# Issuing W1's first half ahead of the mirror matrices, and batch 1's row sums ahead of batch 2's loads, on GpSimd

## The chip, the cores and the metric

The kernel runs on one core of one Trainium2 chip. The metric is the device time of one execution in microseconds (us). The engines are named as in the profile: PE (TensorE matmuls), PEld (its weight loads), DVE (VectorE), ACT (ScalarE), POOL (GpSimd) and SP (SyncE, which here only issues DMAs).

## The reference, cut to what matters

```python
scores = (1 / sqrt(64)) * q @ k.T                # 8 batches, 12 heads, 448 rows, 64 columns
attn   = maximum(scores, 0) ** 2 / 448
x      = (attn @ v) laid out as (8, 448, 768)    # heads side by side
mixed  = real(fft(fft(x, axis=1), axis=2))       # Fourier mixing over rows and columns
u      = x + mixed
un     = (u - mean(u)) / sqrt(var(u) + 1e-6)     # per row, over 768 columns
out    = u + maximum(un @ w_ch1, 0) @ w_ch2      # w_ch1: 768 x 3072, w_ch2: 3072 x 768
```

All inputs and the output are float32; the kernel works in bfloat16 for the products.

## The kernel before, in words

**Stages.** For each batch the kernel forms scores and values in pairs of heads (lines 961, 829, 834), brings the result `x` into `xT`, folds it for the Fourier transform (lines 734 to 787), multiplies by cosine and sine tables along the columns (`mix`, line 1439) and along the rows (`mix_rows`, line 1251). `mix_rows` then adds `x` to the mixed rows: its inner generator `rows(i)` makes `u`, the mean and variance, and the normalised `un`. A half of 128 or 112 rows has two mirrored parts: `i = 0` is summed on DVE and `i = 1` on POOL (lines 1282 and 1284, two instructions each). For batch 1 `un` is made on ACT (line 1310), and then turned on PE against a unit or a mirror matrix (line 1212, `turn_rows`) into `unT`, the input of the feed-forward product. Batch 0 has a path of its own, `first_tail`, in which POOL makes `un` at line 1109 for three of the four parts; it needs the mirror matrix `rev` on PE.

**Feed-forward.** The rows of all batches are cut into groups. `ffn` multiplies a group by W1 (line 1937), applies the maximum (line 1924 on ACT, line 1922 on DVE) and multiplies by W2 (line 1965 for the first group, 1992 and 2078 later), with line 1630 adding the result into the output rows. The later groups reuse sums of weight blocks to save products (lines 1533, 1769, 2078). The first group's second product walks W2 in four quarters and needs each quarter's load.

**The order of the work.** All instructions of an engine run in the order in which a planner, `Streams.run`, lists them when the program is built. Each part of the work is a generator ("stream") that says with `need(engine, time, due times, buffers)` when its next step could start. The planner takes the stream with the least key:

```python
t = [self.engine[eng]] + [d.t if isinstance(d, Cell) else d for d in deps]
...
key = (ok is not None and not ok(), max(t) + HEAD.get((s[3], eng, phase), 0.0), s[1][eng != "PE"])
```

`s[3]` is the name of the generator, `phase` counts which of the planner times 48, 140, 290 and 440 us have passed on PE, and the last entry is a rank that settles equal keys. `HEAD` thus makes one kind of step look earlier than it is, in one phase, on one engine.

**POOL's list.** POOL issues all loads of q, k, v, W1 and W2 through the software DMA queue (q0 in the profile), in the order that `loading` spells out; the stores and reloads of `u`, the transposes and the output go through SP (q1). Before each load the planner waits for the landing of the load eight places back (`ring`), and so does the program itself, which has eight loads in flight at most:

```python
def ring():
    return [landed[-8] + 1.2] if len(landed) > 7 else []
```

A load of a group of four heads is one instruction at line 483 for each of q, k, v (the k and v tiles are called `kn` and `vn`), and two small ones at line 458 for the last quarter of the rows (`load_halves`). `load_w1(0)` and `load_w1(1)` issue six loads each at line 522, `load_w2` two at a time at line 533. Between the loads POOL also makes small constants: `mirrors` (lines 283 to 303) makes `rev`, the index vectors `back` for the mirrored stores of line 1348, and the matrix `order` that `halve` uses at line 415; `seq_table` (lines 365 to 373) makes the angles from which DVE and ACT make the row tables (lines 380 to 390).

Of the kernel before, what the change touches and what calls it, by code (L numbers as in the profile page):

```python
# [61 lines left out]

HEAD = {('attentions', 'PE', 2): -0.6, ('attentions', 'PE', 3): -0.6, ('attentions', 'PE', 4): 0.07, ('mix_rows', 'PE', 2): -0.05}
OVERLAP = {"ACT": 0.12, "DVE": 0.07}
STAGE = [1]
LATENCY = {"PE": 0.28, "ACT": 0.18, "DVE": 0.16, "POOL": 0.2, "SP": 0.1}
# [3 lines left out]
class Streams:  # L72
# [29 lines left out]
    def run(self):  # L102
        end = {}
        while self.streams:
# [10 lines left out]
            for s in self.streams:  # L115
# [6 lines left out]
                for p in set(bufs):  # L122
                    t.append(sorted(p.free)[bufs.count(p) - 1])
                key = (ok is not None and not ok(), max(t) + HEAD.get((s[3], eng, phase), 0.0), s[1][eng != "PE"])
                if best is None or key < best[0]:
# [24 lines left out]
def need(eng, dur, deps=(), bufs=(), ok=None):  # L150
    return eng, dur, list(deps), list(bufs), ok
# [26 lines left out]
def kernel(  # L178
# [21 lines left out]
    NG = H // HG  # L200
# [81 lines left out]
    def mirrors():  # L282
        order[0] = work.tile([128, 128], BF16, name="order", tag="qkr0", bufs=1)
        nc.gpsimd.memset(rev, 0.0)
        nc.gpsimd.affine_select(out=rev, in_=rev, compare_op=ALU.not_equal, fill=1.0,
                                base=-127, pattern=[[1, 128]], channel_multiplier=1)
        nc.gpsimd.iota(back[0], pattern=[[0, 1]], base=HS, channel_multiplier=-1)

        v = const.tile([128, 2], FP32, name="backv")
        nc.gpsimd.iota(v[:, 0:1], pattern=[[0, 1]], base=HS - 128, channel_multiplier=-1,  # L290
                       allow_small_or_imprecise_dtypes=True)
        nc.gpsimd.tensor_scalar(v[:, 1:2], v[:, 0:1], 0.0, float(UB), op0=ALU.is_lt, op1=ALU.mult)
        nc.gpsimd.tensor_tensor(v[:, 0:1], v[:, 0:1], v[:, 1:2], op=ALU.add)
        nc.gpsimd.tensor_copy(back[1], v[:, 0:1])
        for i in range(2):
            nc.gpsimd.iota(back2[i], pattern=[[0, 1]], base=HS - 2 + i, channel_multiplier=-2)
        nc.gpsimd.memset(order[0], 0.0)
        for i in range(2):
            n = EH - i
            nc.gpsimd.affine_select(out=order[0][:, i * EH:i * EH + n], in_=order[0][:, i * EH:i * EH + n],  # L300
                                    compare_op=ALU.not_equal, fill=1.0, base=-i, pattern=[[-2, n]],
                                    channel_multiplier=1)
        nc.gpsimd.tensor_scalar(order[0][:, EH - 1:EH], order[0][:, EH - 1:EH], 0.5, None, op0=ALU.mult)
# [56 lines left out]
    def seq_table():  # L360

        f = work.tile([128, 4 * KH], FP32, name="dfty", tag="uA", bufs=1)
        g = work.tile([128, 4 * KH], FP32, name="dfty", tag="uB", bufs=1)
        yield need("POOL", 0.55)
        nc.gpsimd.iota(drow[:, 0:2], pattern=[[128, 2]], base=0, channel_multiplier=1,
                       allow_small_or_imprecise_dtypes=True)
        nc.gpsimd.iota(dcol[:, 0:SX], pattern=[[1, SX]], base=0, channel_multiplier=0,
                       allow_small_or_imprecise_dtypes=True)
        yield need("POOL", 0.3)
        nc.gpsimd.tensor_scalar(drow[:, 0:2], drow[:, 0:2], 1.0 / S, None, op0=ALU.mult)  # L370
        for i in range(2):
            e = yield need("POOL", 0.45)
            nc.gpsimd.tensor_scalar(f[:, i * SX:(i + 1) * SX], dcol[:, 0:SX], drow[:, i:i + 1], None, op0=ALU.mult)
        f, g = f[:, 0:2 * SX], g[:, 0:2 * SX]
        sch.add(seq_sines(f, g, e + LATENCY["POOL"]), (0, 0.3))

    def seq_sines(f, g, e):

        e = yield need("DVE", 0.4, [e])
        nc.vector.tensor_scalar(g.bitcast(mybir.dt.int32), f, 1.0, None, op0=ALU.mult)  # L380
        yield need("DVE", 0.55)
        nc.vector.tensor_tensor(f, f, g.bitcast(mybir.dt.int32), op=ALU.subtract)
        e = yield need("DVE", 0.4)
        nc.vector.tensor_scalar(g.bitcast(mybir.dt.int32), f.bitcast(mybir.dt.int32), 0x7FFFFFFF, None,
                                op0=ALU.bitwise_and)
        flat = seq.rearrange("p t a s -> p t (a s)")
        for dst, y, sign, bias in ((flat[:, 0], g, -1, halfpi), (flat[:, 1], f, 1, zero_t),
                                   (nseq.rearrange("p a s -> p (a s)"), f, -1, zero_t)):
            e = yield need("ACT", act(2 * SX), [e + LATENCY["DVE"], last_relu])
            nc.scalar.activation(dst, y, AF.Sin, bias=bias, scale=sign * 2.0 * math.pi)  # L390
        seq_ready.t = nseq_ready.t = dft_ready.t = e + LATENCY["ACT"]
# [44 lines left out]
    def ring():  # L436
        return [landed[-8] + 1.2] if len(landed) > 7 else []
# [25 lines left out]
    def load_group(i, which=(0, 1, 2), parts=(0, 1)):  # L463

        b, g = divmod(i, NG)
        hs = slice(g * HG, (g + 1) * HG)
        for x, src in enumerate((q, k, v)):
            if x not in which:
                continue
            if 0 in parts:  # L470
                if b == 0 and x < 2:
                    e = yield need("POOL", 0.75, ring())
                    t = first_qk[x][:R, g] if x == 0 else first_qk[x][:, g]
                else:
                    e = yield need("POOL", 0.75, ring() if b < 3 else [], [BQ[x] if x == 2 else BQ[x][home(i)]])
                    t = (work.tile([R, HG, 4 * Dh], BF16, name="qn", tag=f"qn{home(i)}", bufs=1) if x == 0 else
                         kn_homes[home(i)] if x == 1 else vn_home[:, 3 * g * HG * Dh:3 * (g + 1) * HG * Dh])
                if x == 0:
                    to, j, rows = t, 4, S
                else:  # L480
                    to, j, rows = (t[:, :, 0:3 * Dh] if x == 1 else
                                   t.rearrange("p (h x) -> p h x", h=HG)), 3, KT
                nc.gpsimd.dma_start(out=to, in_=src[b, hs, 0:rows].rearrange("h (p j) d -> p h (j d)", j=j))  # L483
                loads[i][x] = None if x == 2 else t.rearrange("p h (j d) -> p j h d", j=4)
                landed.append(sch.dma(e, GRP * rows / S, 390e3, "sw"))
                arrive(i, x)
            if i == 0 and x == 1:
                e = yield need("POOL", 0.55)
                dft_indices()
                indices_ready.t = e + LATENCY["POOL"]  # L490
                yield need("POOL", 0.6)
                make_identity(nc, ident)
            if x and 1 in parts and (b > 0 or g == x - 1):
                yield from load_halves(b, g if b else 0, 1 if b else NG, x)
            if i == 2 and x == 2:
                yield need("POOL", 0.75)
                pads()
            if i == NG + 1 and x == 1 and 0 in parts:
                yield need("POOL", 3.6)
                mirrors()  # L500


    qk_left = Cell()
    kn_homes = [work.tile([128, HG, 4 * Dh], BF16, name="kn", tag=f"kn{i}", bufs=1) for i in range(QN)]
# [13 lines left out]
    def load_w1(hf):  # L518
        for m in range(MC):
            e = yield need("POOL", 0.6, ring())  # L520
            t = wpool.tile([128, FF // 2], BF16, name=f"w1_{m}_{hf}")
            nc.gpsimd.dma_start(
                out=t, in_=moe_w_ch1[m * 128:(m + 1) * 128, hf * (FF // 2):(hf + 1) * (FF // 2)])
            w1_sb[m][hf] = t
            done = sch.dma(e, 128 * FF * 2, 430e3, "sw")
            landed.append(done)
        w1_ready[hf].t = done
# [11 lines left out]
    def loading():  # L539
        for i in range(NG):  # L540
            yield from load_group(i)

        yield from load_group(NG, (0, 1))
        yield from load_group(NG + 1, (0, 1), (0,))
        yield from load_w1(0)
        yield from seq_table()
        yield from load_group(NG + 1, (1,), (1,))
        yield from load_w1(1)
        for i in (NG, NG + 1):
            yield from load_group(i, (2,), (0,))  # L550
        yield from load_halves(1, 0, 2, 2)
        yield from load_group(NG + 2, (0, 1))
        yield from load_w2(range(2))
        yield from load_group(NG + 2, (2,))
        yield from load_w2(range(2, 4))
        for i in range(2 * NG, B * NG):
            yield from load_group(i)
# [931 lines left out]
    rows = out.rearrange("b s d -> (b s) d")  # L1489
# [732 lines left out]
```

## Time and profile before

| | us |
|---|---|
| three runs | 570.31, 567.71, 572.16; median 570.31 |
| the profiled execution's own time | 570.35 |
| its span, first to last instruction | 568.4 |
| PE busy | 557.1 (98% of the span), granted clock 0.999 |
| DVE, ACT, POOL busy | 436.4, 318.4, 194.4 |
| software queue q0 | 33.63 MB, 44.1% of 16 engines' span |
| hardware queue q1 | 48.09 MB, 38.7% |

The span runs from the first to the last instruction of the program; 1.95 us of the execution's time lie outside it. PE is the engine that carries the span, and the columns of the views that matter below are: a start time in us from the span's start, a duration, the engine, the line and its tiles, and in brackets the engine's idle time before the instruction and what ended it.

### The profile page before, as it was taken

What the parts mean: (1) busy time and instruction counts of PE and PEld (TensorE: products, weight loads), DVE (VectorE), ACT (ScalarE), POOL (GpSimd) and SP (SyncE); (2) the same over time, 40 slices, a digit from 0 to 9 for tenths busy, and PEclk for the clock granted to TensorE, in tenths of its full rate; (3) what the DMA queues carried; (4) which work ended last, traced back from release to release, by engine and by line L of the source; (5) the groups of instructions that cost most, each with busy time, mean ns of one, the idle gap of its engine ahead of it and who ended that gap; (6) DMA issues with size and microseconds to landing.
All of it is one profiled execution on the core that took longest, in us unless ns stands there. A gap on an engine that the chain in (4) does not pass through costs nothing.

```text
span 568.4 us, 11147 instructions
## 1 busy us (share of the span) xinstructions
PE 557.1 (98%) x4171; PEld 350.0 (62%) x4171; DVE 436.4 (77%) x1015; ACT 318.4 (56%) x537; POOL 194.4 (34%) x281
## 2 busy tenths in 40 slices
PE   8999998899999999999999999999999999999997
PEld 4475555544455555546756756767678688668864
DVE  7977563887789977887998897878899957644762
ACT  6978762677745676676786647638615164015400
POOL 8965223524336234462445545322005000000000
PEclk9999999999999999999999999999999999999999
DMA  9999999999968987899799989957425421231012
GB/s 113 175 210 233 201 219 150 220 152 119 176 94 219 210 137 157 163 184 211 163 160 206 191 126 160 194 128 154 115 65 167 117 87 29 71 124 57 1 57 83
DMA packets 152688, 82.41 MB, mean 145 GB/s; under 512 B 118076, under 2 KB 147900, under 8 KB 152636
## 3 DMA queue, kind: packets, MB, share of 16 engines
q0 software_dynamic: 57056, 33.63, 44.1%
q1 hardware_dynamic: 95580, 48.09, 38.7%
q8 instruction: 32, 0.52, 0.4%
q14 instruction: 20, 0.16, 0.1%
HBM read 62.91 MB, written 26.25 MB: 157 GB/s over the span
## 4 chain that ended last, share of the span: by engine, by line
PE 87%; DMA 6%; DVE 2%; ACT 2%; POOL 1%; issue 1%; DVEq 0%; POOLq 0%; ACTq 0%
PE psF L1937 25%; PE psF L2078 21%; PE psS L1769 8%; PE psS L961 8%; DMA kn<-in_k_dram 6%; PE psS L2078 5%; PE psF L834 5%; PE psF L1992 4%; PE psS L1439 2%; PE psF L1769 2%; PE psF L1965 2%; PE psF L829 1%; PE psF L630 1%; PE psS L834 1%; PE psS L1247 1%
## 5 line engine op out<-in xcount | busy, mean ns | idle before, releaser
L1937 PE MATMUL psF<-unT,w 128*128 128x256 bf16 (+2 forms) x1152 | 165.3, 299 | 0.0
L974 ACT ACTIVATE sq<-psS 128x896 bf16<-128x896 f32 x168 | 144.1, 920 | 31.7 <-PE psS L961 31.4
L1937 PEld LDWEIGHTS <-w 128*128 128x128 bf16 x1152 | 110.9, 98 | 49.6 <-issue 5.2
L991 DVE TENSOR_TENSOR sq<-sq 128x896 bf16<-128x896 bf16 x144 | 89.4, 638 | 13.8 <-ACT sq L974 13.2
L2078 PEld LDWEIGHTS <-hT 128*128 128x128 bf16 x648 | 62.4, 98 | 44.2 <-issue 4.6
L1924 ACT ACTIVATE hT<-psF 128x512 bf16<-128x512 f32 (+2 forms) x121 | 59.6, 508 | 41.4 <-PE psF L1937 39.3
L1630 DVE TENSOR_TENSOR o<-psF,o 128x384 f32<-128x384 f32 (+1 forms) x78 | 42.6, 547 | 23.5 <-PE psF L2078 19.8
L2078 PE MATMUL psF<-w,hT 128*128 128x384 bf16 x336 | 59.9, 326 | 0.7 <-DVE o L1630 0.6
L961 PE MATMUL psS<-qkT 64*128 64x448 bf16 (+1 forms) x336 | 51.5, 355 | 0.4 <-DVE qkT L637 0.3
L1784 ACT COPY copies<-psS 128x256 f32<-128x256 f32 x57 | 19.9, 374 | 53.1 <-PE psS L1769 48.0
L696 DVE TENSOR_SCALAR xT<-psF 128x224 bf16<-128x224 f32 x60 | 20.6, 384 | 26.8 <-PE psF L834 26.8
L1282 POOL TENSOR_TENSOR u<-tp,xn 112x385 f32<-112x385 f32 (+2 forms) x14 | 14.3, 1019 | 72.9 <-DVE tp L1262 49.3
L483 POOL DMA_DIRECT2D qn<-in_q_dram x21 | 15.7, 747 | 58.9 <-DVE qkr L590 51.4
L834 PE MATMUL psF<-sq,vn 128*64 128x448 bf16 x246 | 33.0, 362 | 0.0
L961 PEld LDWEIGHTS <-qkT 64*128 64x128 bf16 (+1 forms) x336 | 12.9, 94 | 31.7 <-issue 26.4
L1769 PEld LDWEIGHTS <-w 128*128 128x128 bf16 x288 | 28.2, 98 | 4.7 <-issue 1.1
L458 POOL DMA_DIRECT2D kn<-in_k_dram x42 | 25.7, 621 | 12.1 <-DMA w<-in_moe_w_ch_dram 8.0
L1291 DVE BATCH_NORM_STATS2 stats<-u 112x6 f32<-112x384 f32 (+2 forms) x56 | 28.7, 543 | 0.9 <-POOL u L1282 0.7
L458 POOL DMA_DIRECT2D vn<-in_v_dram x42 | 26.1, 637 | 5.9 <-DMA w<-in_moe_w_ch_dram 5.1
L483 POOL DMA_DIRECT2D vn<-in_v_dram x24 | 18.9, 787 | 25.5 <-PE psS L961 25.4
L1310 ACT ACTIVATE un<-u,small 112x768 bf16<-112x768 f32 (+2 forms) x22 | 22.0, 1023 | 10.0 <-DVE small L1297 8.6
L1965 PE MATMUL psF<-w,hT 128*128 128x384 bf16 x144 | 24.9, 326 | 1.5 <-DMA w<-in_moe_w_ch_dram 1.5
(239 smaller groups left out, 936.6 us busy)
## 6 DMA issues: line engine op xcount, KB each, us to landing
out_dram<-o SPq DMA_DIRECT2D x55, 192.0 KB, 2.1
qn<-in_q_dram POOLq DMA_DIRECT2D x21, 224.0 KB, 5.1
vn<-in_v_dram POOLq DMA_DIRECT2D x24, 192.0 KB, 5.6
w<-in_moe_w_ch_dram POOLq DMA_DIRECT2D x12, 384.0 KB, 10.6
w<-in_moe_w_ch_dram POOLq DMA_DIRECT2D x4, 1152.0 KB, 22.6
kn<-in_k_dram POOLq DMA_DIRECT2D x21, 192.0 KB, 5.6
utop<-u SPq DMA_DIRECT2D x12, 336.0 KB, 3.1
o<-utop SPq DMA_DIRECT2D x16, 192.0 KB, 3.7
```

The costliest lines, as they stand in the source:

```text
L458: nc.gpsimd.dma_start(out=t[par * Dh:(par + 1) * Dh, par::2], in_=at)
L483: nc.gpsimd.dma_start(out=to, in_=src[b, hs, 0:rows].rearrange("h (p j) d -> p h (j d)", j=j))
L834: nc.tensor.matmul(av[h * Dh:(h + 1) * Dh, 0:S], lhsT=vn_home[:, at:at + Dh], rhs=sq[:, h, :], start=start, stop=stop, skip_group_check=True)
L961: nc.tensor.matmul(sc[:, h, 0:S].rearrange("k (c q) -> k c q", c=4), lhsT=flat[ps, k0:k0 + KB], rhs=qT[ps, pair], start=True, stop=True)
L974: nc.scalar.activation(r, sc[:, :, 0:S], AF.Relu)
L991: nc.vector.tensor_tensor(r, r, r, op=ALU.mult)
L1630: nc.vector.tensor_tensor(o[:, cols], pc[:, cols], o[:, cols], op=ALU.add)
L1769: nc.tensor.matmul(ps[:, 0:N], lhsT=lhs, rhs=rhs[:, m], start=(start and m == 0), stop=(stop and m == 2), skip_group_check=True)
L1924: nc.scalar.activation(hs, ps, AF.Relu)
L1937: nc.tensor.matmul(ph[:, i * N:(i + 1) * N], lhsT=w1_sb[m][hf][:, (jj + i) * 128:(jj + i + 1) * 128], rhs=unT[:, m, 0:N], start=(m == 0), ...
L1965: nc.tensor.matmul(pc[:, 0:DH], lhsT=block(j, c), rhs=w2(j, hf), start=(j == 0), stop=(j == JC - 1))
L2078: nc.tensor.matmul(pc[:, cols], lhsT=lhs[i], rhs=rhs[i][:, cols], start=(start and i == 0), stop=(i == KP - 1), skip_group_check=True)
```

## The change

It has two parts. `mirrors` is called from `loading` directly behind `load_w1(0)`, where before it was called from `load_group` ahead of it, behind the k load of batch 1's second group: POOL's thirteen instructions for the mirror matrices come behind W1's first six loads. And the steps named `rows` get a head of 1.5 us on POOL in phase 1, which covers the row sums of batch 1.

```diff
-HEAD = {..., ('mix_rows', 'PE', 2): -0.05}
+HEAD = {..., ('mix_rows', 'PE', 2): -0.05, ('rows', 'POOL', 1): -1.5}
@@ load_group
-            if i == NG + 1 and x == 1 and 0 in parts:
-                yield need("POOL", 3.6)
-                mirrors()
@@ loading
         yield from load_group(NG + 1, (0, 1), (0,))
         yield from load_w1(0)
+        yield need("POOL", 3.6)
+        mirrors()
         yield from seq_table()
         yield from load_group(NG + 1, (1,), (1,))
         yield from load_w1(1)
```

More of the change, by code (lines that the diff above doesn't have):

```diff
@@ L61, in give @@
         self.ids.append((when, self.tiles.pop(id(t))[1]))
[L65 removed]
+HEAD = {('attentions', 'PE', 2): -0.6, ('attentions', 'PE', 3): -0.6, ('attentions', 'PE', 4): 0.07, ('mix_rows', 'PE', 2): -0.05, ('rows', 'POOL', 1): -1.5}
 OVERLAP = {"ACT": 0.12, "DVE": 0.07}
```

## The prediction

> **What bounds the kernel now.** I read the page first (PE busy 557.1 of 568.4 us), then the windows view, cut where PE stands idle, then the timelines of PE, DVE, ACT and POOL in those stretches. In the windows the first number is the stretch, the second PE's busy time.
>
> ```profile
> 20.00:88.00 68.00, 67.32 (x575) 38.24 (x572) 47.44 (x117) 50.25 (x83) 32.59 (x51) 1.00 1.17 208
> 88.00:106.00 18.00, 14.92 (x100) 9.24 (x99) 10.03 (x25) 5.41 (x8) 11.93 (x17) 1.00 1.60 147
> 106.00:545.00 439.00, 437.59 (x3203) 280.73 (x3202) 353.87 (x817) 247.67 (x428) 131.67 (x163) 1.00 0.76 139
> ```
>
> PE is the bound at full granted clock, and the change takes no product away. Only PE's idle time can move: 0.68 us from 20 to 88, 3.08 from 88 to 106, 1.41 from 106 to 545. The 3.08 are two waits, in PE's timeline:
>
> ```profile
> 90.34 2.11 PE L1965 MATMUL psF<-w,hT 128*128 128x384 bf16 x12 [1.51 <-DMA w<-in_moe_w_ch_dram]
> 93.62 9.91 PE L1965 MATMUL psF<-w,hT 128*128 128x384 bf16 x60
> 105.10 0.51 PE L1212 MATMUL psS<-ident,un 128*128 128x128 bf16 x6 [1.57 <-ACT un L1310]
> ```
>
> The first group's second product waits 1.51 us for the last quarter of W2. Then `turn_rows` waits 1.57 us for batch 1's first `un`, with a product behind it that needs nothing from it. Each part of the change lies upstream of one of these waits.
>
> **First part: W1 ahead of the mirrors.** POOL's timeline, and the DMA issues that start in stretches around single loads (last number: us from issue to landing):
>
> ```profile
> 17.43 0.82 POOL L483 DMA_DIRECT2D kn<-in_k_dram  x1
> 18.17 0.29 POOL L284 MEMSET rev<- 128x128 bf16 x1
> 21.01 3.33 POOL L522 DMA_DIRECT2D w<-in_moe_w_ch_dram  x6
> 25.30 2.65 POOL L373 TENSOR_SCALAR dfty<-early,drow 128x240 f32<-128x240 f32 x2
> 30.95 0.54 POOL L522 DMA_DIRECT2D w<-in_moe_w_ch_dram  x1 [0.64 <-DMA w<-in_moe_w_ch_dram]
> 32.67 0.54 POOL L522 DMA_DIRECT2D w<-in_moe_w_ch_dram  x1 [1.18 <-DMA w<-in_moe_w_ch_dram]
> ...
> kn<-in_k_dram POOLq DMA_DIRECT2D x1, 192.0 KB, 5.3
> w<-in_moe_w_ch_dram POOLq DMA_DIRECT2D x1, 384.0 KB, 4.9
> w<-in_moe_w_ch_dram POOLq DMA_DIRECT2D x1, 1152.0 KB, 32.1
> kn<-in_k_dram POOLq DMA_DIRECT2D x1, 16.0 KB, 4.4
> ```
>
> The four DMA rows are the k load of 17.43, W1's first piece of 21.01, W2's last quarter (the second of the two issued from 57.37, so at 58.2) and the small k load of 52.17. The mirrors hold POOL from 18.17 to 21.01, 2.84 us in which nothing is issued. The k load lands at 17.43 + 5.3 = 22.7, the first W1 piece at 21.01 + 4.9 = 25.9. When W1 flows, POOL gets a free place every 1.8 us (30.95 to 32.67), so a piece takes 1.8 us. Issued at 18.17, the first piece would land at the later of 18.17 + 4.9 = 23.1 and 22.7 + 1.8 = 24.5: 1.4 us sooner, not 2.84. The windows view says the same in bytes (last column GB/s):
>
> ```profile
> 21.00:24.00 3.00, 3.00 (x22) 0.95 (x18) 2.96 (x8) 3.00 (x4) 2.99 (x7) 1.00 0.88 114
> 27.00:30.00 3.00, 3.00 (x20) 1.45 (x18) 2.93 (x10) 2.28 (x5) 3.00 (x5) 1.00 1.08 212
> ```
>
> 98 GB/s are missing for 3 us, which at 212 GB/s is 1.39 us. Does this head start live until W2? The queue lands in order with eight loads in flight, POOL itself waits for landings from 30.95 on, and the loads behind inherit the shift in issue and in landing. It dies if the queue runs dry. The closest point that I find is the small k load of 52.17, which lands after 4.4 us; an unqueued load of this kind takes 2.7 (the least in the view of line 458):
>
> ```profile
> DMA to landing us min/median/max: 2.7/5.2/22.0
> ```
>
> So 1.7 us of queue were still ahead of it, more than the 1.39. W2's last quarter then lands at 58.2 + 32.1 - 1.35 = 88.95 instead of 90.3, and PE, which comes at 88.83, waits 0.15 instead of 1.51. I take **-1.35 us**; the bounds are 0 (head start used up by the SP queue's traffic) and -1.51 (the whole wait).
>
> What is late by it: the six W1 issues themselves, because the loads eight places back (issued from 14.1 to 16.8) land some 5 us after issue; I estimate the sixth issue 0.7 us later than six in a row would be. The mirrors and `seq_table` move to 25.0 and 28.6. Their users:
>
> ```profile
> 28.66 0.40 DVE L380 TENSOR_SCALAR dfty<-dfty 128x480 int32<-128x480 f32 x1
> 35.44 0.33 PE L1039 MATMUL psS<-rev,xT 128*128 128x128 bf16 x3
> 38.39 0.97 POOL L1109 TENSOR_SCALAR un<-u,small 128x768 bf16<-128x768 f32 x1
> 40.99 0.50 PE L1137 MATMUL psS<-ident,un 128*128 128x128 bf16 x6
> ```
>
> DVE comes to the table at 28.66, some 0.1 us before POOL's new end plus a signal. `rev` is first used at 35.44, ten us later. Both cost nothing; without that cover the table would cost 0.7. In the planner the due times of W1 come nearly 2.8 us forward, so both small v loads of line 458 may stand ahead of the first `un` of line 1109, and POOL would wait there for a free place until about 39. That `un` would end near 40.5. Its cover is PE, which asks for it at 40.99: nothing, with 0.4 us to spare. What is late there up to 0.15 us more would only fill the remaining W2 wait.
>
> **Second part: row sums ahead of loads.** POOL, DVE and ACT before the second wait:
>
> ```profile
> 98.44 0.77 POOL L483 DMA_DIRECT2D qn<-in_q_dram  x1
> 99.89 0.67 POOL L458 DMA_DIRECT2D kn<-in_k_dram  x1
> 100.51 1.00 POOL L1282 TENSOR_TENSOR u<-tp,xn 128x385 f32<-128x385 f32 x1
> 101.39 0.92 POOL L1284 TENSOR_TENSOR u<-qs,xn 128x383 f32<-128x383 f32 x1
> ...
> 93.70 0.43 DVE L590 COPY qkr<-qn 112x1024 bf16<-112x1024 bf16 x1 [7.81 <-DMA qn<-in_q_dram]
> 95.75 0.43 DVE L590 COPY qkr<-kn 128x1024 bf16<-128x1024 bf16 x1 [1.17 <-DMA kn<-in_k_dram]
> 98.69 0.55 DVE L1284 TENSOR_TENSOR u<-tp,xn 128x383 f32<-128x383 f32 x1
> 101.54 0.56 DVE L1291 BATCH_NORM_STATS2 stats<-u 128x6 f32<-128x384 f32 x1 [0.67 <-POOL u L1282]
> 102.33 0.56 DVE L1291 BATCH_NORM_STATS2 stats<-u 128x6 f32<-128x384 f32 x1 [0.23 <-POOL u L1284]
> 103.66 0.32 DVE L1297 SCALAR_TENSOR_TENSOR small<-small 128x1 f32<-128x1 f32 x1
> ...
> 104.02 1.95 ACT L1310 ACTIVATE un<-u,small 128x768 bf16<-128x768 f32 x2 [0.55 <-DVE small L1297]
> ```
>
> The `un` that PE waits for comes from DVE's own sum (i = 0), but in DVE's list its last scaling (103.66) stands behind the statistics of POOL's sum, and those waited 0.67 + 0.23 = 0.90 us for POOL. POOL had loads of batch 2 in front. A head of 1.5 us moves the sums ahead of one or two loads, as each load is planned at 0.75; I take the two behind the q load of 98.44 (0.77 + 0.67 with their overlap put the sums at 99.2, 1.3 us sooner). DVE then no longer waits: **-0.90 us**. The chain in front of it starts from landings (the idle 7.81 and 1.17 at DVE's copies), which the first part brings forward by the same 1.35 as PE, so the two gains add. Bounds: 0 and -1.57 (the whole wait, if DVE's list is also dealt better).
>
> Behind the sums now stand the k loads of batch 2's third group, and all of batch 2's rest. They go out about 3.8 us later (four sums); its first reader is DVE's copy:
>
> ```profile
> 119.85 0.42 DVE L590 COPY qkr<-kn 128x1024 bf16<-128x1024 bf16 x1
> ```
>
> A load issued at 103 that takes the 8 to 9 us which these take lands by 112, its halves two later: 6 us of cover, cost nothing; without it 3.8.
>
> **The sum** is made against the profiled execution, 570.35 (span 568.4 and 1.95 around it; the median of the runs is 570.31, so the two agree): 570.35 - 1.35 - 0.90 = **568.1 us**.
>
> **The rivals.**
>
> *The sums collide with DVE's sums.* Where POOL's and DVE's row sums ran at the same time, batch 2's, POOL's from 167.39, DVE's were stretched:
>
> ```profile
> 167.39 0.91 POOL L1282 TENSOR_TENSOR u<-tp,xn 113x385 f32<-113x385 f32 x1 [5.08 <-DVE tp L1262]
> 167.93 0.78 DVE L1282 TENSOR_TENSOR u<-qs,xn 113x385 f32<-113x385 f32 x1
> 168.63 1.19 DVE L1284 TENSOR_TENSOR u<-tp,xn 113x383 f32<-113x383 f32 x1
> ```
>
> 0.78 + 1.19 against twice 0.55: 0.87 us. In this kernel DVE's sums for batch 1 ran alone (to 99.24). If POOL's start two loads sooner than I take, at 98.44 or before, the chain to `un` gains 0.90 and loses 0.87: 570.35 - 1.35 - 0.03 = 569.0. Against it: from 99.2 on only 0.05 us overlap. Chance 0.13. The Trainium skill, SBUF: State Buffer, section "Who interferes with whom", says that a DVE instruction with two SBUF inputs and a GpSimd instruction that reads SBUF exclude each other for a whole instruction, whichever starts first; the rows above agree in kind. By that rule DVE's pair would end with POOL's pair (98.44 + 1.92 = 100.36 against 99.24), 1.12 us, and the time would be 569.2.
>
> *The head start is lost.* The hardware queue's transfers take it up between 37 and 90, and W2 lands at 90.3 as before. Then only the second wait shrinks: 569.45. For it: from 88 to 106 the DMA share is 1.60 at only 147 GB/s, so the queues crowd each other. Against it: bytes that leave early leave room later. Chance 0.17.
>
> *The change does nothing that shows.* Both waits are set by other work, 570.35; chance 0.05.
>
> *PE's list is dealt worse (the slower side).* The planner believes the sums sooner and may list the first `turn_rows` (L1212) earlier among line 1965's products. Six of these take 9.91 / 60 x 6 = 0.99 us. If it moves ahead of two of them (1.5 us of head allow one or two) while PE gains 1.35 at W2 but the copies' landings do not, `un` comes only 0.90 sooner: the end moves by -0.90 + 2 x 0.99 = +1.08, to 571.4. It decides from the first product on, if the real `un` gains less than PE loses. Against it: in the trace `un` hangs on DVE's list, which POOL does not lengthen. For it: the list from there on is worked out anew, and the same kind of move can recur at each later batch. Chance 0.20.
>
> **How the numbers follow.** Forecast 0.45, rivals 0.13, 0.17, 0.05, 0.20. The forecast's own range is 567.3 (both waits gone, -3.08) to 569.5. The range to be given reaches from 567.3 less 1.3, half of the 2.6 by which the lowest of the three runs lies under their median, to 571.4 and 0.6 above it: 566.0 to 572.0; what is left out is mainly the repeated case of the last rival. About 1% (5.7 us) is what a measurement of this kernel can tell from no change. Faster by that would need more than the idle time from 20 to 545 (5.17 us): 0.05. Slower by that needs the last rival six times over in later batches, half of its chance: 0.10. Within 1%: 0.85.
>
> **What would show it.** After: W1's first issue near 18.2; the stretch from 21 to 24 near 200 GB/s; PE's wait for W2 under 0.4 us near 89; POOL's sums next behind one q load; no DVE wait for POOL at line 1291; PE's wait at L1212 near 0.7 us; no new wait over 0.5 us after 106. Wrong would be: W2 landing still at 90, DVE's row sums longer than 0.6 us, L1212 with a wait over 1.6 us, or idle time from 106 to 545 well above 1.41.

## The result, and the profile after

The change makes the kernel slower: 572.63 us against 568.54 us, medians of 18 runs each; ratio 1.0058, 95% interval 1.0039 to 1.0076. The profiled execution of the changed kernel took 573.98 us, its span is 572.0. Line numbers of the changed kernel beyond line 500 are 2 to 4 lower than before (L1628 is L1630, L1963 is L1965, L1210 is L1212).

The fences below are single rows of the views, in order of time. The windows view after, first with all engines (the first pair behind the stretch is PE), then a second answer with PE alone, whose last columns are the granted clock, the DMA share and GB/s:

```profile
20.00:88.00 68.00, 66.45 (x573) 37.97 (x572) 47.73 (x117) 50.70 (x83) 33.99 (x57) 1.00 1.20 210
88.00:106.00 18.00, 15.01 (x86) 8.50 (x84) 11.35 (x21) 4.03 (x7) 12.94 (x18) 0.93 1.55 195
106.00:545.00 439.00, 436.43 (x3194) 280.01 (x3195) 354.76 (x818) 247.79 (x428) 130.05 (x162) 1.00 0.73 137
...
21.00:24.00 3.00, 3.00 (x20) 1.00 1.24 202
100.00:106.00 6.00, 3.29 (x12) 0.78 1.30 273
106.00:120.00 14.00, 13.89 (x100) 0.97 0.74 155
120.00:165.00 45.00, 43.75 (x250) 1.00 0.92 130
165.00:545.00 380.00, 378.80 (x2848) 1.00 0.71 137
```

PE's idle time went from 0.68 to 1.55 us between 20 and 88, from 3.08 to 2.99 between 88 and 106, and from 1.41 to 2.57 from 106 to 545. That is 1.94 of the 3.6 us between the two spans. The rest goes by the clock: from 100 to 120 us PE works at a granted clock of 0.78 and 0.97, which is 6 x 0.22 + 14 x 0.03 = 1.74 us of lost work. Before, the clock there was 1.00. From 165 on nothing has changed. Of the 18 runs, seven have a mean granted clock of 0.997 or less; the other eleven still have a median of 571.2, so the clock is a part of the loss and not all of it. PE's timeline:

```profile
57.57 0.39 PE L628 MATMUL psF<-ident,qn 112*64 112x112 bf16 x8 [0.58 <-ACT hT L1922]
88.33 2.11 PE L1963 MATMUL psF<-w,hT 128*128 128x384 bf16 x12
102.53 3.29 PE L1963 MATMUL psF<-w,hT 128*128 128x384 bf16 x12 [2.62 <-DVE o L1628]
106.11 0.78 PE L1210 MATMUL psS<-ident,un 128*128 128x128 bf16 x6 [0.30 <-ACT un L1308]
152.79 0.35 PE L827 MATMUL psF<-sq,vn 128*128 128x448 bf16 x1 [1.13 <-DVE hT L1920]
```

Both waits that the forecast counted on are gone or small: 88.33 runs on without a wait for W2, L1210 waits 0.30 instead of 1.57. In their place stands a wait of 2.62 us for an output add, after which twelve products take 3.29 us instead of 2.11; and there are two new waits of 0.58 and 1.13 us elsewhere. DVE and POOL tell where the 2.62 come from. First DVE's timeline of the changed kernel:

```profile
94.90 0.43 DVE L588 COPY qkr<-kn 128x1024 bf16<-128x1024 bf16 x1 [3.18 <-DMA kn<-in_k_dram]
95.24 0.55 DVE L1628 TENSOR_TENSOR o<-psF,o 128x384 f32<-128x384 f32 x1
97.83 0.97 DVE L1280 TENSOR_TENSOR u<-qs,xn 128x385 f32<-128x385 f32 x1
98.72 3.29 DVE L1282 TENSOR_TENSOR u<-tp,xn 128x383 f32<-128x383 f32 x1
101.93 0.55 DVE L1628 TENSOR_TENSOR o<-psF,o 128x384 f32<-128x384 f32 x1
104.83 0.16 DVE L1295 SCALAR_TENSOR_TENSOR small<-small 128x1 f32<-128x1 f32 x1
```

Then POOL's:

```profile
88.54 0.72 POOL L483 DMA_DIRECT2D qn<-in_q_dram  x1 [6.17 <-DMA w<-in_moe_w_ch_dram]
98.18 0.80 POOL L483 DMA_DIRECT2D kn<-in_k_dram  x1
98.95 0.97 POOL L1280 TENSOR_TENSOR u<-tp,xn 128x385 f32<-128x385 f32 x1
99.83 0.89 POOL L1282 TENSOR_TENSOR u<-qs,xn 128x383 f32<-128x383 f32 x1
100.63 0.95 POOL L1280 TENSOR_TENSOR u<-tp,xn 112x385 f32<-112x385 f32 x1
101.50 1.20 POOL L1282 TENSOR_TENSOR u<-qs,xn 112x383 f32<-112x383 f32 x1
```

DVE's second sum, 0.55 us of work, started at 98.72 and ended at 102.01. POOL ran three sums back to back in that time, and DVE came through only as the fourth began. The first sum of DVE's pair took 0.97 instead of 0.55 too, while POOL by the profile was still issuing loads; why is not shown. The output add of 101.93, which frees the PSUM bank that PE waits for, stands behind it.

How the instructions of the two kernels are listed matters for all that follows. In the traces the changed kernel's order differs from the one before not only on POOL, but also on PE, DVE, ACT and SP: the planner works with due times, the first part brings W1's due times nearly 2.8 us forward, and so it deals everything else anew. On PE one group of six products of L1937 falls from 55 to 83 us, groups of L1965 around `turn_rows` change places, and a group of L1937 moves near 140 us. On DVE the output add (95.24) now stands behind the copy of kn; it stood ahead of it (94.04, before 95.75).

### The profile page after: what moved, and what is told of

It is laid out like the page before. It is cut to its first block, busy times and chain, and to the rows that moved or that the text cites. A ratio compares the mean times of both kernels' runs of the same rounds, so it can differ in the third digit from the quotient of the medians.

```text
span 572.0 us, 11142 instructions
## 1 busy us (share of the span) xinstructions
PE 558.7 (98%) x4170; PEld 350.4 (61%) x4170; DVE 440.7 (77%) x1017; ACT 317.6 (56%) x535; POOL 194.9 (34%) x281
## 4 chain that ended last, share of the span: by engine, by line
PE 78%; DMA 9%; POOL 4%; DVE 4%; ACT 2%; issue 1%; SPq 1%; DVEq 0%; POOLq 0%; ACTq 0%
PE psF L1935 22%; PE psF L2076 21%; PE psS L1767 8%; PE psS L959 6%; PE psS L2076 5%; DMA kn<-in_k_dram 5%; PE psF L1990 4%; DMA vn<-in_v_dram 4%; PE psF L832 3%; PE psS L1437 2%; PE psF L1767 2%; PE psF L1963 2%; DMA qkT<-qkr 1%; PE psF L827 1%; PE psS L832 1%
## 5 line engine op out<-in xcount | busy, mean ns | idle before, releaser
L2076 PE MATMUL psF<-w,hT 128*128 128x384 bf16 x336 | 59.9, 326 | 0.7 <-DVE o L1628 0.6
L1628 DVE TENSOR_TENSOR o<-psF,o 128x384 f32<-128x384 f32 (+1 forms) x78 | 42.6, 547 | 22.9 <-PE psF L2076 19.7
L1963 PE MATMUL psF<-w,hT 128*128 128x384 bf16 x144 | 26.4, 336 | 2.8 <-DVE o L1628 2.8
```

The lines of the kernel that those rows point to most:

```text
L1628: nc.vector.tensor_tensor(o[:, cols], pc[:, cols], o[:, cols], op=ALU.add)
L1963: nc.tensor.matmul(pc[:, 0:DH], lhsT=block(j, c), rhs=w2(j, hf), start=(j == 0), stop=(j == JC - 1))
L2076: nc.tensor.matmul(pc[:, cols], lhsT=lhs[i], rhs=rhs[i][:, cols], start=(start and i == 0), stop=(i == KP - 1), skip_group_check=True)
```

## The experiments

Each kernel was timed against the kernel before on the same chip. "Slow clock" counts the runs whose mean granted clock was 0.997 or less, that is, in which more than 1.4 us were lost to it. The runs of before in the sets of e1 to e16 have 4 of 121.

| run | what is in it | median us | ratio, 95% interval | slow clock |
|---|---|---|---|---|
| after | the whole change | 572.63 | 1.0058 (1.0039 to 1.0076) | 7 of 18 |
| e1 | first part, planner told | 571.83 | 1.0065 (1.0035 to 1.0096) | 5 of 12 |
| e2 | second part | 568.18 | 1.0003 (0.9991 to 1.0015) | 0 of 12 |
| e3 | first part, planner not told | 568.09 | 1.0009 (0.9990 to 1.0029) | 2 of 12 |
| e4 | both parts, planner not told of the first | 568.12 | 1.0009 (0.9989 to 1.0029) | 1 of 12 |
| e5 | e1, `turn_rows` one group later | 569.52 | 1.0037 (1.0017 to 1.0057) | 2 of 10 |
| e6 | e1, copy of kn on POOL | 572.74 | 1.0073 (1.0044 to 1.0101) | 3 of 6 |
| e7 | e3, `turn_rows` one group earlier | 568.65 | 1.0023 (1.0008 to 1.0038) | 1 of 12 |
| e8 | e3, `un` 4 us late | 574.77 | 1.0117 (1.0098 to 1.0136) | 5 of 5 |
| e9 | e1, transpose behind the store | 570.75 | 1.0050 (1.0028 to 1.0072) | 3 of 12 |
| e10 | e5 and e9 together | 570.81 | 1.0051 (1.0033 to 1.0068) | 0 of 11 |
| e11 | whole change, transpose behind the store | 573.15 | 1.0077 (1.0043 to 1.0111) | 4 of 8 |
| e12 | e3, transpose ahead of the store | 568.01 | 0.9999 (0.9986 to 1.0012) | 0 of 11 |
| e13 | the plan of e1, no work moved | 571.56 | 1.0049 (1.0025 to 1.0073) | 4 of 12 |
| e14 | planner's figure 2.25 us, no work moved | 570.89 | 1.0037 (1.0020 to 1.0055) | 2 of 12 |
| e15 | planner's figure 3.4 us, no work moved | 570.21 | 1.0018 (1.0000 to 1.0036) | 1 of 12 |
| e16 | whole change without POOL's sums of batch 1 | 569.37 | 1.0002 (0.9989 to 1.0016) | 0 of 12 |

**Which part costs it (e1 to e4).** e1 is the first part of the diff alone, e2 the second alone. In e3 the instructions of the mirrors are emitted behind W1's first six loads, but the planner's charge for them stays where it was, so that every list but POOL's is that of the kernel before (the traces of e2 and e3 show this order on every engine but POOL); e4 adds the second part to that.

```diff
@@ e3: load_group, the charge stays
                 yield need("POOL", 3.6)
-                mirrors()
@@ e3: loading
-        yield from load_w1(0)
+        yield from load_w1(0); mirrors()
```

> Only the first part: mirrors behind W1's first half, no head for the row sums. The lists of PE, DVE, ACT and SP are those of the changed kernel but for small swaps; POOL's sums of batch 1 stand one small load later. Collision theory (DVE's second row sum was held to 3.29 us by POOL's sums, which the two parts together brought up to 98.95): here POOL's sums start near 99.6, after DVE's pair has ended near 98.9, that pair takes 0.55 each again, PE's 2.6 us wait for the output add at line 1630 is gone, ratio to before 0.995 to 0.998. Re-deal theory (the lists that W1's earlier due times re-dealt cost the time, above all DVE's copy of kn ahead of the output add): the loss stays, ratio 1.003 to 1.006.

> Only the second part: the head of 1.5 us for the row sums. All lists are those of before but for one small k load that goes behind POOL's sums, which start 0.6 us sooner, near 99.9; DVE's pair ended at 99.24 before. Collision theory: too late to collide, DVE waits 0.6 us less at line 1291, ratio 0.998 to 1.000; if the pair collides after all, DVE's second sum is stretched and the ratio is above 1.003. Re-deal theory: nothing is re-dealt, ratio 0.999 to 1.000.

> Only the head start of W1, with every list but POOL's kept as before: POOL issues W1's first six loads and then makes the mirrors, while the planner counts the 3.6 us of the mirrors where they were. Head-start term of the prediction: W2's last quarter lands 1.4 to 2.0 us sooner, PE's wait at line 1965 near 89 falls from 1.51 to under 0.2, the time falls by 1.3 to 1.6 us, ratio 0.997. If the head start is lost on the way: ratio 1.000. Re-deal theory needs this one to be faster than e1 by 0.5% or more; by the collision theory the two are within 0.2%.

> Head start of W1 with the lists of before, and the head for the row sums, which moves one small k load behind them: the two effects that the prediction summed, without the re-dealt lists. By the prediction's sum: 2.0 to 2.3 us less than before, ratio 0.996. By the collision theory this holds only as far as POOL's sums start after DVE's pair; if DVE's second sum is over 1 us here, the ratio is 1.000 or more. Re-deal theory: 0.996.

Moving W1 ahead of the mirrors gains nothing and costs nothing as long as the lists are those of before, and neither does the second part. e1 alone loses as much as the whole change. Its profile, though, has no collision: POOL's sums began at 99.33, when DVE's were over. PE's timeline of e1:

```profile
103.88 0.51 PE L1212 MATMUL psS<-ident,un 128*128 128x128 bf16 x6 [2.45 <-ACT un L1310]
104.22 3.24 PE L1965 MATMUL psF<-w,hT 128*128 128x384 bf16 x12
```

A wait of 2.45 us for `un`, and again slow products behind it. The theory that the collision alone is the cause fell here. e3's profile has a cost of its own: POOL finishes the angle table later, DVE waits for it, and PE waits for DVE. The timeline of e3, first DVE, then PE:

```profile
30.01 0.41 DVE L380 TENSOR_SCALAR dfty<-dfty 128x480 int32<-128x480 f32 x1 [1.22 <-POOL dfty L373]
...
31.81 0.26 PE L1414 MATMUL psS<-chan,fold 128*128 128x193 bf16 x1 [0.46 <-DVE fold L755]
```

The same wait of PE, 0.46 or 0.47 us, stands in e7, e8 and e12, which have e3's order on POOL; it is not in e4. The profile of e2, which leaves the issue of W1 and W2 as before, also tells something of the forecast's first term; PE's timeline:

```profile
89.15 2.11 PE L1965 MATMUL psF<-w,hT 128*128 128x384 bf16 x12
103.70 0.51 PE L1212 MATMUL psS<-ident,un 128*128 128x128 bf16 x6 [1.36 <-ACT un L1310]
```

There is no wait for W2. In the five profiles with W1 behind the mirrors as before it is 1.51 us (before), 0.66 (e15) and none (e2, e13, e14): it differs from one execution to the next.

**Where PE stands when it asks for `un` (e5, e7).** In e1's list the amount of work ahead of the first `turn_rows` of batch 1 is one group of six products (0.99 us) less than before. e5 puts it back, e7 does the opposite to e3; nothing else moves on any engine. The products are held back and emitted behind the next group:

```diff
@@ e5: turn_rows, first of batch 1
-        for m in range(MC): nc.tensor.matmul(pt..., lhsT=un..., rhs=idn, ...)
+        held.append(products)
@@ e5: ffn, behind the next six products of L1965
+        while held: held.pop()()
```

> The first part alone (571.83, 1.0065), with one edit on TensorE: the first six products of L1212 (the turned rows of batch 1) stand behind the next six products of L1965 instead of ahead of them; every other list is that of the first part alone. Place theory (TensorE asks for un one group of 0.99 us too early): the wait at L1212 falls from 2.45 to about 1.4 us, the granted clock stays at 1.00 between 100 and 120 us in most runs, and the median falls by 1.0 us of wait and by some of the 1.7 us of slow clock, to 570.0 to 570.8. Early-stage rival (the loss stems from 20 to 60 us, where GpSimd's mirror matrices and small loads stand otherwise): 571.8 as before, since nothing there changes. DVE rival (the output add behind the copy of kn): 571.8 as well.

> W1's loads first with the lists of the kernel before (568.09, 1.0009), and one edit on TensorE: the first six products of L1212 stand one group of six L1965 products (0.99 us) earlier, as in the changed kernel; every other list is untouched. Place theory: un stood ready 0.6 us or less ahead of TensorE in that profile, so a wait of 0.4 to 1 us more appears at L1212, more in executions where the load of kn is late; median 568.5 to 569.2, ratio 1.001 to 1.003, and some runs with a slow clock. Early-stage rival: nothing, 568.1, as the early lists are those of before.

PE's timeline of e5, then of e7:

```profile
103.96 0.51 PE L1213 MATMUL psS<-ident,un 128*128 128x128 bf16 x6 [1.72 <-ACT un L1312]
...
103.98 0.51 PE L1212 MATMUL psS<-ident,un 128*128 128x128 bf16 x6 [2.16 <-ACT un L1311]
```

Both went the way of the place theory: e5 falls from 1.0065 to 1.0037, e7 rises from 1.0009 to 1.0023. The intervals of each pair overlap, so the size stays rough. Place is not all: e5 still loses.

**What a wait costs by itself (e8).**

```diff
-                nc.scalar.activation(un[:n], u[:n], AF.Identity, ...)
+                for _ in range(5 if (b, ch, i) == (1, 0, 0) else 1):
+                    nc.scalar.activation(un[:n], u[:n], AF.Identity, ...)
```

> W1's loads first with the lists of the kernel before, and one edit on ScalarE: the first un of batch 1 (L1310, 0.97 us) is computed five times in a row instead of once, which is 3.9 us later for the same result; it measures what a wait at L1212 costs by itself. TensorE reached L1212 at 102.01 with un ready at about 101.1, so it should wait about 2.9 us. If a wait costs only itself: 568.1 + 2.9 = 571.0 and a mean granted clock of 1.00. If a wait of over about 2.4 us makes the granted clock fall behind it, as the profiles of the changed kernel and of its first part alone showed (0.78 to 0.92, 1.7 us lost): 572 to 573, with the clock of the whole run at 0.997 or less in most runs.

The loss is 1.17%, some 6.6 us, for about 4 us of delay. PE's timeline of e8:

```profile
106.74 0.82 PE L1212 MATMUL psS<-ident,un 128*128 128x128 bf16 x6 [4.58 <-ACT un L1311]
107.35 2.13 PE L1966 MATMUL psF<-w,hT 128*128 128x384 bf16 x6
```

Six products that take 1.14 at full clock take 2.13. In this execution kn had landed later than in e3's profile, so PE waited 4.58 and not 2.9; every one of its timed runs has a slow clock. Put side by side, the profiles draw a line. Waits of 1.72 (e5), 2.05 (e15), 2.16 (e7) and 2.27 us (e9) left the clock at 1.00. PE's timeline and windows of e9:

```profile
103.87 0.51 PE L1213 MATMUL psS<-ident,un 128*128 128x128 bf16 x6 [2.27 <-ACT un L1311]
100.00:106.00 6.00, 3.73 (x27) 1.00 1.64 141
106.00:120.00 14.00, 14.00 (x99) 1.00 1.04 237
```

Waits of 2.45 (e1), 2.48 (e13), 2.62 (after), 2.70 (e11) and 4.58 us (e8) were followed by a loss of 1.74, 1.68, 1.74, 1.70 and 1.68 us, each worked out as 6 x (1 - clock from 100 to 106) + 14 x (1 - clock from 106 to 120). In e6 (3.85 us) it was 3.42, twice as much. Cut into single microseconds, the clock stands at 0.50 for 3.4 us in each of these, and for 6.8 in e6. The fall does not come at a fixed point of the wait: in e13 it comes 2.3 us after the wait began, in e8 4.5 us after, in e1 1.1 us after the wait had ended. So the length of a wait alone does not say when the clock falls. The Trainium skill, TensorE: Matmul & The Clock Gate, Part 1, says that a window of about 3.4 us without work halves the clock until a busy window of that length has passed. Its price, half of 3.4, agrees with the 1.7 us here; the length of wait does not, as 2.45 us were enough.

**DVE held by a load that nobody needs soon (e6).** In e1 DVE stood for 3.89 us until kn landed at 94.91, with batch 1's row work queued behind its copy.

```diff
-                    nc.vector.tensor_copy(o, loads[b * NG + g][x])
+                    (nc.gpsimd if (b, g, x) == (2, 0, 1) else nc.vector).tensor_copy(o, loads[b * NG + g][x])
```

> The first part alone, with one edit: the copy of batch 2's first kn (L590) runs on GpSimd instead of VectorE, so VectorE does not stand still for 3.89 us until kn has landed at 94.91 while batch 1's row work (L1262 onward) is queued behind it. Theory (VectorE held by a load that nobody needs soon is what makes un late at L1212): VectorE starts L1262 when qs is there, near 93.5 instead of 95.87, un comes some 2 us earlier, the wait at L1212 falls from 2.45 to below 0.6, no slow clock there, median 569.0 to 570.0. Early-stage rival: 571.8. GpSimd's copy may share its port with VectorE and stretch some of L1262 to L1284; if that decides, the gain is below 1 us.

The expectation missed. DVE's row work did start at 91.92, but it then met the next wait. The profile is of the slowest of its six runs (576.74). The timeline of e6, first DVE, then POOL, then PE:

```profile
94.51 0.55 DVE L1284 TENSOR_TENSOR u<-tp,xn 128x383 f32<-128x383 f32 x1
101.08 0.56 DVE L1291 BATCH_NORM_STATS2 stats<-u 128x6 f32<-128x384 f32 x1 [3.40 <-POOL u L1282]
...
97.02 1.07 POOL L590 COPY qkr<-kn 128x1024 bf16<-128x1024 bf16 x1
98.00 0.75 POOL L483 DMA_DIRECT2D qn<-in_q_dram  x1
100.08 0.97 POOL L1282 TENSOR_TENSOR u<-tp,xn 128x385 f32<-128x385 f32 x1
...
104.65 0.82 PE L1212 MATMUL psS<-ident,un 128*128 128x128 bf16 x6 [3.85 <-ACT un L1310]
```

DVE's scalings for `un` stand behind the statistics of POOL's sums, and POOL's sums stand behind the copy and the loads. The 4 us that DVE gained at L1262 (95.87 in e1) became a wait of 3.40 us for POOL, and with the copy in front POOL came 0.75 us later than in e1 (99.33). Two chains arrive at `un` nearly together; taking one away shows the other.

**The transpose beside kn's landing (e9 to e12).** In the re-dealt lists the DMA transpose of batch 2's first qn is issued at 91 to 92 us, ahead of the first output store, while kn is still landing, and in the profiles up to here kn's copy followed qn's by 3.6 to 4.4 us against 2.0 to 2.5 in most profiles with the old lists (3.7 in e4). e9 and e11 put it back behind the store, e10 adds e5's edit, e12 does the opposite to e3:

```diff
@@ e9: turning, batch 2's first group
-                    nc.sync.dma_start_transpose(out=parts[x], in_=qk[x])
+                    for y in ([x] if (b, g) != (2, 0) else [0, 1] if x else []):
+                        nc.sync.dma_start_transpose(out=parts[y], in_=qk[y])
```

> The first part alone (571.83, 1.0065), with one edit on SyncE: the DMA transpose of batch 2's first qn (L600) is issued behind the first output store of L1610, as in the kernel before, instead of ahead of it; every other list is that of the first part alone. Crowding theory: in the lists of the change that transpose starts at 91.2, while kn is still landing, and kn's copy follows qn's copy by 3.6 to 4.4 us instead of 2.0 to 2.5; with the transpose later the gap falls to about 2.3, VectorE starts batch 1's row work some 2 us earlier, the wait at L1212 falls from 2.45 to 0.3 to 0.8 us, and the median to 569.2 to 570.2. Rival (kn is late because GpSimd issued it 1 us later): the gap stays above 3.5 and the median at 571.8.

> Both repairs at once on the first part alone: the transpose behind the output store, and TensorE's first six products of L1212 one group of L1965 later. Crowding and place theory together: no wait over 0.3 us at L1212, clock 1.00; what is left is the 0.6 us wait of L630 for ScalarE's hT near 58 and some 0.3 us near 37, so 568.6 to 569.4, ratio 1.001 to 1.002. If the transpose is innocent: 569.5 as with the place alone.

> The whole change (1.0058), with the one edit on SyncE of the run before (transpose behind the output store). TensorE's L1212 stands where it stood before in the lists of the whole change, so this is the kernel of both repairs plus GpSimd's row sums ahead of one small load. If the row sums cost nothing by themselves: 568.6 to 569.4 as there. If their collision with VectorE's sums (3.29 us for one of them in the profile of the change) comes in most executions: 1 to 2 us more, 570 to 571.

> W1's loads first with the lists of the kernel before (1.0009), and the opposite edit on SyncE: the transpose of qn ahead of the output store, so right behind qn's copy. Crowding theory: kn's copy follows qn's by 3.6 us or more instead of 2.5, VectorE's row work starts 1 to 2 us later, a wait of 0.5 to 1.5 us stands at L1212 and the median goes up to 568.6 to 569.5. Rival: nothing, 568.1.

This theory fell. e9 still waits 2.27 us at `turn_rows`; the gap in e9 is 3.1 us, in e10 4.1 and in e11 3.6 with the transpose late, and e12, where it is early, loses nothing at 568.01. e10 shows a repair being paid back; PE's timeline:

```profile
101.92 0.51 PE L1214 MATMUL psS<-ident,un 128*128 128x128 bf16 x6
107.13 0.74 PE L962 MATMUL psS<-qkT 64*128 64x448 bf16 x6 [1.02 <-DMA qkT<-qkr]
```

No wait is left at the first products of `turn_rows`, but the transpose that was put off is now waited for. e10 loses 1.0051 with no slow clock in 11 runs: PE's idle time from 20 to 545 us is 5.16 us against 2.56 in e3's profile, 1.02 of it here and 0.91 at a wait for hT near 149. So a re-dealt list can lose without a late `un`. e11 brought something else: it repeats the collision of the changed kernel. DVE's timeline of e11, then PE's:

```profile
97.99 1.04 DVE L1283 TENSOR_TENSOR u<-qs,xn 128x385 f32<-128x385 f32 x1
98.95 3.32 DVE L1285 TENSOR_TENSOR u<-tp,xn 128x383 f32<-128x383 f32 x1
...
102.78 3.06 PE L1966 MATMUL psF<-w,hT 128*128 128x384 bf16 x12 [2.70 <-DVE o L1631]
```

Both profiles with the whole change's own lists and POOL's sums have it; the others, e4 with both parts and the old lists among them, do not. The head of 1.5 us moved POOL's sums past one small load of 0.6 us and no more, and that small load had kept them behind DVE's.

**The lists alone (e13 to e15).** In these no work moves at all; only the planner's figure for the mirrors does. e13 charges it behind W1, which gives the lists of e1 on PE, DVE, ACT and SP with POOL's mirrors where they were; the other two change the figure in its old place, which leaves the first 50 us nearly alone (e14) or everything up to the group of L1937 near 140 us (e15).

```diff
@@ e15: load_group
-                yield need("POOL", 3.6)
+                yield need("POOL", 3.4)
                 mirrors()
```

> The kernel before with none of the change's work moved: GpSimd makes the mirror matrices ahead of W1 as before. Only the planner's 3.6 us for them are charged behind W1, so that its lists are those of the first part of the change (152 differing rows on TensorE, 49 on VectorE). Re-deal theory: the loss is in the lists and not in the moved work, so 571 to 572, ratio 1.005 to 1.007, with the 0.6 us wait of L630 for hT near 58, the wait at L1212 and the wait of L829 for hT near 150. Rival (the moved mirrors and loads cost it): 568.1, ratio 1.000 to 1.002.

> The kernel before with the planner's figure for the mirror matrices set to 2.25 us instead of 3.6, and nothing else: no work moves, the lists are those of the run before from 50 us on (the products of L1937, L1965 and L1212 and what follows near 150), but its first 50 us are dealt almost as in the kernel before. Re-deal theory: most of the loss, ratio 1.003 to 1.006. If the first 35 us carry it: 1.000 to 1.002.

> The kernel before with the planner's figure for the mirror matrices set to 3.4 us instead of 3.6: one group of six products of L1937 stands earlier near 150 us on TensorE, VectorE's and SyncE's rows around it move with it, and all ahead of it is untouched. This part of the re-deal alone: a wait of 0.5 to 1.1 us of L829 for hT near 150 as in the changed kernel (1.13), ratio 1.001 to 1.002. If it is covered: 1.000.

This settles where the loss of the first part is: 1.0049, 1.0037 and 1.0018, with not one instruction of the mirrors or of W1 moved. The more of the list is dealt anew, the larger it is, though the three intervals overlap and e15's begins at 1.0000. The wait of 0.5 to 1.1 us near 150 that was expected of e15 is not in its profile, in which PE's idle time from 120 to 165 is 0.56 us against 0.20 before; whether e15 loses is open. In e14's profile PE waits 1.52 us at `turn_rows`, at full clock, 1.81 between 20 and 88 and 1.10 between 120 and 165 (e3: none, 1.16 and 0.20), so `turn_rows` is not the only place that costs. The profile of e13 has e1's signature; PE's timeline of e13:

```profile
104.51 0.82 PE L1212 MATMUL psS<-ident,un 128*128 128x128 bf16 x6 [2.48 <-ACT un L1310]
```

And its windows, PE alone:

```profile
100.00:106.00 6.00, 3.52 (x22) 0.86 1.69 138
106.00:120.00 14.00, 14.00 (x95) 0.94 0.85 222
```

**Without POOL's sums (e16).**

```diff
-            eng.tensor_tensor(u[:n, 0:KN], ts[i][:n, 0:KN], x[:n, 0:KN], op=ALU.add)
+            (eng.memset(u[:n, 0:KN], 1.0) if b == 1 and i == 1 else eng.tensor_tensor(u[:n, 0:KN], ...))
```

> The whole change (1.0058), but GpSimd fills its four sums of batch 1's rows (L1282, L1284) with constants instead of adding; the sums are left out. Lists and waits are those of the change. Collision theory: VectorE's L1284 takes 0.55 instead of 3.29 us, TensorE's wait of 2.6 us at L1965 for the output add goes, and no slow clock follows it; 570 to 571, ratio 1.003 to 1.005 (what the lists cost is left). If the collision is no part of the usual loss: 572.6 as the change.

Here more went than expected: not only the collision's share but, as far as can be measured, all of the loss: 1.0002, with an interval that leaves room for 0.9 us. DVE's timeline of e16, then PE's:

```profile
95.18 0.43 DVE L590 COPY qkr<-kn 128x1024 bf16<-128x1024 bf16 x1 [3.21 <-DMA kn<-in_k_dram]
98.58 0.55 DVE L1284 TENSOR_TENSOR u<-tp,xn 128x383 f32<-128x383 f32 x1
101.95 0.16 DVE L1297 SCALAR_TENSOR_TENSOR small<-small 128x1 f32<-128x1 f32 x1
...
103.22 0.51 PE L1212 MATMUL psS<-ident,un 128*128 128x128 bf16 x6 [1.09 <-ACT un L1310]
```

From the copy of kn to the end of the scaling for `un` it is 6.9 us here, 7.85 in e1 (94.91 to 102.76) and 10.1 in the changed kernel (94.90 to 104.99). With the chain that short PE's wait stays at 1.1 us, the clock stays up in all twelve runs, and the same re-dealt lists cost nothing that can be measured. So in the whole change the loss shows by how late `un` comes against the place where PE asks for it, and POOL's sums have a part in how late that is. Which part is the collision's is not shown: POOL's four steps take 1.55 us here and 3.75 with the sums, so all that stands behind them on POOL starts earlier as well.

No version came out ahead of the kernel before: e2, e3, e4, e12 and e16 equal it, and e16 leaves sums out.

## Why the prediction was wrong, step by step

The step that failed is the term put at nothing, the re-dealt lists. The forecast took 2.25 us off for the two moves and nothing on for the lists. e4, which makes both moves with the lists of before, measures 1.0009, so the moves gain nothing that can be measured; e13, which moves no work and only deals the lists anew as the first part does, measures 1.0049.

**The base of the sum.** It was made against one execution of 570.35 us with a wait of 1.51 us for W2. The median of before in the later sets of runs is 567.7 to 568.6, and e2's profile shows no such wait with W1 and W2 issued as before; two of the three times that were shown, 570.31 and 572.16, lie 2 to 4 us above that median. The term of -1.35 was worked out correctly as a mechanism: 21 to 24 us moves 202 GB/s as predicted, W1's first issue is at 18.21, and W2's last piece had landed when POOL went on at 88.54, where the forecast had 88.95. With the lists of before up to there, POOL goes on at 90.59 (before), 89.18 (e2) and 90.58 (e15) with W1 behind the mirrors, and between 87.01 and 89.16 with W1 ahead (e3, e4, e7, e8, e12), so the head start does reach W2. But it removes a wait that not every execution has, and e3 measures the gain as nothing; its interval leaves 0.6 us at most.

**The costs put at nothing.** `rev` was covered as argued. The table was not: DVE waited 0.85 us for it in the changed kernel and 1.22 in e3, where PE then waited 0.46 for the fold behind it. The mirrors took 4.26 us instead of 2.84. DVE's squares ran beside them from 23.45 to 26.77 us; POOL's steps that read a tile in that time took about twice as long or more, while those that only write, and those outside that time, took what they took before. The longest steps in POOL's timeline after,

```profile
24.72 0.46 POOL L294 CAST backs<-backv 128x1 int32<-128x1 f32 x1
25.57 1.31 POOL L300 TENSOR_SCALAR_AFFINE_SELECT order<-order 128x57 bf16<-128x57 bf16 x2
```

took 0.18 and 0.57 before. e3 has the same stretch (1.31 at L300) and the wait for the table, and shows no loss, so neither makes the loss of the change. What does make it had been mentioned and put at nothing: "In the planner the due times of W1 come nearly 2.8 us forward". I followed that to two small loads at 39 us and not through the other engines' lists.

**The second term.** POOL's sums did come behind fewer loads, as the step said, but past one small load and not past two; DVE no longer waited for POOL at L1291, as the step said; and the 0.90 us were not gained, because DVE's own sums paid for it. In e2, where nothing collides, the term measures nothing either (1.0003).

**The collision rival** named the right place and mechanism and was mis-sized: 0.87 us forecast from batch 2's rows, 3.29 + 0.97 - 2 x 0.55 = 3.16 measured. In the rows of batch 2 each DVE sum meets one POOL sum; here POOL had four in a row. The rule of the Trainium skill, SBUF: State Buffer, section "Who interferes with whom", by which DVE's pair would end with POOL's first pair and 1.12 us be lost, was as far off: DVE's sum, which by the profile began ahead of POOL's first, waited through three. The point from which it decides was wrong too: sums at 98.95 were enough, DVE's slower first sum having pushed the second to 98.72.

**The rival on PE's list** had the right sign and cause and only a part of the place. It had only `turn_rows` move on PE and said that nothing on POOL's side would lengthen DVE's list. In the whole change `turn_rows` stands behind as much work as before; in e1 it stands one group earlier, and e5 and e7 show what that costs. The loss was in the whole deal, in the profile of the changed kernel against that of before: 0.87 us of waits before 88, 1.16 after 106, and the stretch between.

**What no term had** was the granted clock. The forecast took full clock as given, because it was 1.00 in every window. It stayed so only where PE's waits were short; in these profiles 1.57 us of wait left a margin of about 0.9 us.

## What to carry to other kernels

Where lists are dealt by a planner, a change of any due time is a change of every list behind it: first compare the lists, or move the instruction without telling the planner, and only then price the move itself. A wait seen in one execution is a term of the sum only if other executions have it. And a wait on the engine that sets the end has a second price once it is long enough for the clock to fall, so by these profiles one wait of 2.6 us can cost more than two of 1.3.

## What the runs showed of the hardware

A two-input DVE sum of 0.55 us that meets a row of POOL sums can be held through several of them: 3.29 and 3.32 us in two kernels, though by the profile it had started ahead of POOL's first (98.72 and 98.95 us; 98.95 and 99.20). Here it was not an exchange of one instruction each. Who was first is not certain: the sum before it was stretched too, to 0.97 and 1.04 us, before POOL's first is shown to start.

The granted clock fell after PE waits of 2.45 us and more and not after 2.27 and less, in ten profiles; each fall cost 1.7 us (twice that after 3.85 us), which for a wait of 2.5 us is two thirds of the wait again. That the limit lies between 2.27 and 2.45 us everywhere is not shown: these waits all stand at nearly the same place of the same kernel, and the fall comes at different points of them.

Left open: why kn lands 2 us behind qn in some executions and 4 or 5 in others; in how many executions the collision comes, as it was seen in two profiles, and five of the changed kernel's 18 runs lie under 570 us; and what share of the re-dealt lists' loss stems from the waits of 0.6 us near 58 and of up to 1.1 us near 150. e16 has the first and 0.20 us of the second and loses nothing measurable, while e10 has both and loses 1.0051 at full clock.
